# One kernel for banded attention, a Fourier mix and a feed-forward layer: the first batch's stores on three queues, and a new list schedule

## The chip, the cores and the metric

The kernel runs on one core of a Trainium2 chip. The metric is device time in microseconds, the median of several executions. Engines are named as in the profile: PE (TensorE, matmuls), PEld (its weight loads), DVE (VectorE), ACT (ScalarE), POOL (GpSimd), and SP (SyncE), which only issues transfers.

## What is computed

```python
# q, k, v: (8, 8, 576, 64) float32; w_ch1: (512, 2048); w_ch2: (2048, 512)
scores = q @ k.T / 8                      # per batch and head
mask_plain = (rel >= 0) & (rel < 32)                       # heads 0 to 3, rel = query - key
mask_dil = (rel >= 0) & (rel < 128) & (rel % 4 == 0)       # heads 4 to 7
x = softmax(where(mask, scores, -1e9)) @ v                 # -> (8, 576, 512), heads side by side
u = x + real(fft(fft(x, axis=1), axis=2))                  # along the sequence, then the channels
un = (u - mean(u)) / sqrt(var(u) + 1e-6)                   # along the channels
out = u + relu(un @ w_ch1) @ w_ch2
```

The weights come as 64-bit floats and are narrowed to 32 bits on the chip.

## The kernel before

**Stages.** For each of 8 batches: attention in four head pairs of two units each (`attend`; units are numbered 0 to 63, eight to a batch), where a unit multiplies queries and keys (line 681), masks and reduces on DVE (716), takes exponentials on ACT (722), transposes (736) and multiplies by the values (757, 770). Batch 0 begins with its dilated heads. Their scaled rows (`xt`, lines 797 and 801) are stored to DRAM in an order that folds the sequence (`xsp`, `xsm`, function `store`) and loaded back as half sequences (`fold`, line 570 for both). The plain heads of batch 0 stay in SBUF. `mix` then folds (lines 921 to 945, partly on POOL), multiplies by cosine and sine tables along the sequence (972, 994) and the channels (1018, 1024), adds (885, 887 on POOL), normalises (850 to 862) and writes the rows `us`. The tables' low halves are made on line 635.

Products are of 32-bit floats split in a high and a low part, so each takes three matmuls.

**Feed-forward.** The first 6 of 16 hidden blocks are a filler that runs beside attention and mix of later batches: `fill` takes pairs of row tiles through `up` (line 1152) and `down` (1168), with 12 weight tiles that `prep` loads and narrows (ACT 1090 and 1109, DVE 1092 to 1099, POOL 1111). The other ten blocks come last, as products of 2 x 2 blocks with fewer multiplications (lines 1434, 1532, 1499), ending with the rows left over in the last chunk (`late_down8`, `finish8`, DVE line 1518, `write_out`).

**What sets the order.** Every operation is handed to a `Plan` with an engine, an estimated cost, a priority (lower first) and what it reads and writes. `Plan.run` is a list schedule: it walks an assumed clock, and at each moment an engine takes the first of its ready operations by priority for which buffers are free. The order so found is written out per engine, and each engine runs its stream in order; the assumed times have no part in the program, only the order has. Priorities are built from the constants at the head of the file: a batch's attention lies at 12 b and above; `P_QK0`, `P_V0`, `P_ST0`, `P_FD0`, `P_MIX0` and `P_SPAN0` shift loads, stores, folded loads and mix of batch 0, `P_W` and `P_WF` the filler's 12 weight tiles, `P_FILL` and `P_FILLT` the filler itself. `Q_ST0` names the queues of batch 0's stores in turn (S for SP, A for ACT, P for POOL).

**Spins.** Where PE has nothing else by the planner's clock, it runs pairs of matmuls on a zero tile (line 605, priority 900, up to 250 pairs). Once the first bank of tag "ff" has been taken, the rest of them are dropped:

```python
            if o.prio == SPIN and turn["ff"]:
                o.cost, o.fn = 0.0, lambda: None
```

**Gangs.** PE changes its tiling between attention's score and value matmuls and all others. From unit `NG2` on the two units of a head pair issue their scores directly behind each other (`mate`), and their values too. From unit `NGANG` on a unit's scores also wait for the transposed copy of the unit two before.

## Time and profile before

| | |
|---|---|
| median of 3 runs (1012.09 to 1015.26) | 1012.46 us |
| the profiled execution: its time | 1010.0 us |
| its span, first to last instruction | 1008.2 us |
| PE busy | 997.2 us (99%) |
| DVE busy | 740.8 us (73%) |
| ACT busy | 480.3 us (48%) |
| POOL busy | 297.3 us (29%) |
| granted PE clock | 1.000 |

Busy times are unions of the instructions' spans; for PE the spins count as busy. Matmuls are pipelined, so one matmul's own duration is longer than the distance to the next.

### The profile page before, as it was taken

Reading aid. Unit: us, or ns where it says so; the run is one execution under the profiler, and the core shown is the slowest. Engines: PE = TensorE matmul, PEld = TensorE weight load, DVE = VectorE, ACT = ScalarE, POOL = GpSimd, SP = SyncE. Lnnn points to the kernel's source line nnn. Section 1 sums busy time; section 2 is a strip of 40 time slices with the busy share of each in tenths; the row PEclk is TensorE's granted clock in tenths of the full one; section 3 lists DMA queues with packets and bytes.
Section 4 is the critical chain, followed back from the end, with each engine's and each line's share of the span. In section 5 each row is a group of like instructions: output and inputs, shape, how many; then the busy total and the mean of one; then the engine's idle time right before and its main releaser. Section 6 shows DMA issues by size and latency. Waiting matters only on the chain.

```text
span 1008.2 us, 22155 instructions
## 1 busy us (share of the span) xinstructions
PE 997.2 (99%) x8381; PEld 893.3 (89%) x8381; DVE 740.8 (73%) x2131; ACT 480.3 (48%) x1190; POOL 297.3 (29%) x347
## 2 busy tenths in 40 slices
PE   9999999999999999999999999999999999999998
PEld 8888788989888999899898989899999999999987
DVE  5789987678777656978779776858585858585846
ACT  5776765465746332534435534344343535252522
POOL 1746563526253535474133301010010101010200
PEclk9999999999999999999999999999999999999999
DMA  9968678568864334525546032323232323232211
GB/s 323 305 176 245 206 222 223 161 169 227 225 189 125 113 106 111 168 74 168 158 135 189 32 74 95 74 95 74 87 81 84 85 84 84 84 85 84 84 63 42
DMA packets 92010, 136.31 MB, mean 135 GB/s; under 512 B 9598, under 2 KB 53871, under 8 KB 91904
## 3 DMA queue, kind: packets, MB, share of 16 engines
q1 hardware_dynamic: 88688, 126.77, 43.1%
q0 software_dynamic: 2688, 7.03, 2.3%
q8 instruction: 65, 1.06, 0.5%
q10 hardware_dynamic: 528, 1.11, 0.3%
q14 instruction: 41, 0.34, 0.1%
HBM read 97.66 MB, written 37.21 MB: 134 GB/s over the span
## 4 chain that ended last, share of the span: by engine, by line
PE 91%; DVE 5%; ACT 1%; issue 1%; POOL 1%; DMA 1%; DVEq 0%; SPq 0%; POOLq 0%; ACTq 0%
PE bank L1434 24%; PE bank L1532 20%; PE bank L1152 14%; PE bank L1168 13%; PE bank L1018 4%; PE bank L770 3%; PE bank L972 3%; PE bank L736 3%; PE bank L681 3%; PE bank L605 2%; PE bank L1499 1%; DVE pm L716 1%; PE bank L994 1%; DMA ut<-us 1%; ACT pm L722 1%
## 5 line engine op out<-in xcount | busy, mean ns | idle before, releaser
L1434 PE MATMUL bank<-low,wb 128*128 128x512 f32 x1080 | 255.6, 389 | 0.0
L1434 PEld LDWEIGHTS bank<-low,wb 128*128 128x128 f32 x1080 | 198.1, 188 | 36.9
L1152 PE MATMUL bank<-ut,low 128*128 128x256 f32 x1296 | 169.9, 283 | 0.3 <-DVE low L1160 0.2
L1152 PEld LDWEIGHTS bank<-ut,low 128*128 128x128 f32 x1296 | 159.2, 189 | 3.1 <-DVE low L1160 0.7
L1168 PE MATMUL bank<-low 128*128 128x512 f32 x648 | 161.0, 395 | 0.2 <-DVE low L1160 0.2
L1196 POOL DMA_INDIRECT ut<-us,flip_sb x20 | 41.1, 2053 | 375.1 <-DVE ut L1253 208.5
L1168 PEld LDWEIGHTS bank<-low 128*128 128x128 f32 x648 | 117.2, 188 | 22.9 <-DVE low L1160 0.7
L1440 ACT ACTIVATE xa<-bank 128x256 f32<-128x256 f32 x90 | 34.4, 382 | 177.7 <-PE bank L1434 177.7
L722 ACT ACTIVATE pm<-pm,mx 128x96 f32<-128x96 f32 x256 | 80.9, 368 | 40.3 <-DVE mx L716 39.3
L1471 DVE TENSOR_TENSOR y<-xa 128x384 f32<-128x384 f32 x45 | 25.1, 557 | 97.3 <-ACT xa L1440 97.0
L1275 DVE STREAM_TRANSPOSE ut<-ut 128x512 f32<-128x512 f32 (+1 forms) x76 | 70.6, 978 | 8.7 <-DMA ut<-us 8.5
L1242 DVE TENSOR_TENSOR ut<-ut,bank 128x512 f32<-128x512 f32 (+1 forms) x136 | 74.0, 553 | 2.1
L1160 DVE SCALAR_TENSOR_TENSOR low<-bank,low 128x256 fp32r<-128x256 f32 x108 | 45.1, 420 | 41.2 <-ACT low L1158 40.8
L1532 PEld LDWEIGHTS bank<-w2s,low 128*128 128x128 f32 x588 | 71.7, 188 | 2.1
L1158 ACT ACTIVATE low<-bank 128x256 fp32r<-128x256 f32 x108 | 41.2, 382 | 66.9 <-PE bank L1152 66.2
L1532 PE MATMUL bank<-w2s,low 128*128 128x256 f32 x588 | 72.1, 278 | 0.0
L716 DVE CUSTOM_DVE_ANT_0 pm<-bank,mask_sb 128x96 f32<-128x96 f32 x256 | 53.2, 249 | 14.9 <-PE bank L681 14.7
L1532 PEld LDWEIGHTS bank<-w2s,hm 128*128 128x128 f32 x483 | 58.9, 188 | 1.7
L1532 PE MATMUL bank<-w2s,hm 128*128 128x256 f32 x483 | 59.2, 278 | 0.0
L1109 ACT CAST low<-y 128x640 fp32r<-128x640 f32 (+1 forms) x50 | 35.8, 716 | 38.0 <-DVE y L1473 23.2
L1532 PE MATMUL bank<-low 128*128 128x256 f32 x420 | 51.5, 278 | 0.0
L1532 PEld LDWEIGHTS bank<-low 128*128 128x128 f32 x420 | 50.5, 188 | 0.8
(181 smaller groups left out, 1787.3 us busy)
## 6 DMA issues: line engine op xcount, KB each, us to landing
qk<-in_qk_dram SPq DMA_DIRECT2D x30, 576.0 KB
vt<-in_v_dram SPq DMA_DIRECT2D x31, 438.8 KB
us<-uc SPq DMA_DIRECT2D x36, 257.0 KB
part<-row SPq DMA_DIRECT2D x36, 256.0 KB
wst<-in_w_dram SPq DMA_DIRECT2D x18, 512.0 KB
ut<-us SPq DMA_DIRECT2D x36, 256.0 KB
ut<-part SPq DMA_DIRECT2D x36, 256.0 KB
ut<-us SPq DMA_DIRECT2D x64, 128.0 KB
```

The source lines that it names most:

```text
L716: nc.vector.tensor_tensor_reduce(prob(i)[ps_], sc()[e][ps_, KB * (i // 2):KB * (i // 2) + KB], mask_sb().bitcast(F32)[ps_, kind], -0.125, ...
L722: add("ACT", 0.265, lambda i=i: nc.scalar.activation(out=prob(i), in_=prob(i), func=AF.Exp, bias=mx()[:, i:i + 1], scale=-1.0), ((mx, i),) ...
L1018: nc.tensor.matmul(ps()[:n, :NEP], lhsT=ys[i]()[:, dt, a, rows], rhs=chn_sb[i]()[:, dt, c], start=(dt == 0 and x == 0), stop=(i == 1 and d ...
L1152: nc.tensor.matmul(z()[:, :n_tok], lhsT=wf()[a][:, kk], rhs=ut()[:, p, kk], start=(kk == 0 and n == 0), stop=(kk == KT - 1 and n == 2),)
L1158: add("ACT", act(n_tok) - 0.05, lambda: nc.scalar.activation(out=h()[:, 0, :n_tok], in_=z()[:, :n_tok], func=AF.Relu), (z,), ((h, 0),), prio)
L1160: add("DVE", dve(n_tok), lambda: nc.vector.scalar_tensor_tensor(h()[:, 1, :n_tok], z()[:, :n_tok], 0.0, h()[:, 0, :n_tok].bitcast(F32), op ...
L1168: nc.tensor.matmul(acc(), lhsT=h()[:, a, P * s:P * s + P], rhs=wf()[:, p], start=(first and n == 0), stop=(last and n == 2),)
L1196: add("POOL", 1.04, lambda: nc.gpsimd.indirect_dma_start(dst(), None, us[idx // 4](), bass.IndirectOffsetOnAxis(ap=flip_sb()[:, 4 * kk + i ...
L1242: add("DVE", dve(C if at in (outer, inner) else TOK1), lambda: nc.vector.tensor_tensor(out=blocks(part())[:, at], in0=blocks(part())[:, at ...
L1275: nc.vector.transpose(out=o[back], in_=x[:, g])
L1434: nc.tensor.matmul(z(), lhsT=wb1[NF1 + 2 * p + f]()[:, a, kk], rhs=ut()[:, x, kk], start=(kk == 0 and n == 0), stop=(kk == KT - 1 and n == 2),
L1532: nc.tensor.matmul(acc()[block // 2][:, TOK1 * (block % 2):TOK1 * (block % 2) + TOK1], lhsT=part(hl, a, i, i + 1), rhs=w2s[p]()[:, j, x], ...
```

## The change

The constants of the list schedule change, and with them the order of nearly everything ahead of the last ten hidden blocks. Batch 0's stores go by turns to POOL, ACT and SP. The seq tables' low halves move to DVE and the channel tables' to POOL (`TAB0`, `TAB1`: nonzero is DVE). The planner's assumptions on transfers change: POOL's start later and land later, and two transfers at a time slow each other by half of their overlap. Some assumed DVE costs rise. In the last chunk the second bank's products come in another order for the last pair of blocks (the whole-width product first), and its last DVE step is cut in two halves of 256 columns, each waiting only for its half of the bank.

```diff
-NPT2, NAV2 = 7, 13
-NGANG = 14
+NPT2, NAV2 = 7, 14
+NGANG = 16
-NMX, NG2 = 2, 36
-TAB0, TAB1 = 0, 3
+NMX, NG2 = 2, 32
+TAB0, TAB1 = 10, 0
-P_QK0, P_V0 = -22.11, 15.13
-P_ST, P_FD, P_WD, P_ST0, P_FD0, P_SPAN0, P_SPAN1 = -6.07, -50.32, -13.32, -9.18, -4.2, 26.34, 14.86
-P_QK, P_V, P_TR, P_MIX, P_SPAN, P_W, P_WF, P_FILL, P_FILLT = 19.35, 41.09, -71.2, -1.02, 10.19, 11.28, 7.1, 43.27, 10.96
-P_MIX0, P_MIX1 = -8.0, 6.45
-P_SEQ, P_CHN = 18.96, 20.71
-T_SEQ, T_CHN = 6.63, 39.16
-Q_ST0, Q_X0 = 'P', 'P'
+P_QK0, P_V0 = -28.96, -13.31
+P_ST, P_FD, P_WD, P_ST0, P_FD0, P_SPAN0, P_SPAN1 = -6.34, -52.48, 5.55, -21.88, 0.36, 3.04, 17.39
+P_QK, P_V, P_TR, P_MIX, P_SPAN, P_W, P_WF, P_FILL, P_FILLT = 15.62, 76.61, -97.91, -7.42, 0.09, 10.33, 7.1, 59.56, 47.29
+P_MIX0, P_MIX1 = -1.17, -2.08
+P_SEQ, P_CHN = 19.63, 37.65
+T_SEQ, T_CHN = 20.53, 34.77
+Q_ST0, Q_X0 = 'PAS', 'P'
...
-                        begin = max(pipe.get(eng, 0.0), end + 1.2)
+                        begin = max(pipe.get(eng, 0.0), end + ((LATE1 if lanes[eng] else LATE0) if eng == "POOL" else 1.2))
                         took = got.nbytes / (PIPE0 if end < T_PIPE else PIPE1)
-                        others = [x for x in pipe if x != eng and pipe[x] > begin]
-                        pipe[eng] = begin + took * (1 + len(others))
-                        for x in others:
-                            pipe[x] += took
-                        done = pipe[eng] + LAND[eng]
+                        pipe[eng] = begin + took
+                        for x in pipe:
+                            both = 0.5 * min(took, pipe[x] - begin)
+                            if x != eng and both > 0:
+                                pipe[eng] += both
+                                pipe[x] += both
+                        done = pipe[eng] + (LAND1 if eng == "POOL" else LAND0)
...
-LAND = {"SP": 1.6, "ACT": 1.6, "POOL": 2.8}
-PIPE0, PIPE1, T_PIPE = 3.2e5, 2.7e5, 55.0
+PIPE0, PIPE1, T_PIPE = 3.05e5, 2.7e5, 55.0
+LAND0, LAND1, LATE0, LATE1 = 0.8, 2.4, 4.5, 2.0
...
-            add("PE", 0.22, turn_over, (blank,), (spin,), SPIN, at=0.4 * n)
+            add("PE", 0.23, turn_over, (blank,), (spin,), SPIN, at=0.4 * n)
...
-            for n, (i, j, at) in enumerate((((0, 1, 1), (1, 0, 0), (4, 5, None)), ((2, 1, 1), (3, 0, 0), (5, 5, None)))[e]):
+            todo = [((0, 1, 1), (1, 0, 0), (4, 5, None)), ((2, 1, 1), (3, 0, 0), (5, 5, None))][e]
+            for n, (i, j, at) in enumerate(todo[2:] + todo[:2] if e and p == NPAIR - 1 else todo):
...
-            add("DVE", dve(C), lambda e=e, u=u, row=row: nc.vector.scalar_tensor_tensor(
-                blocks(row()), blocks(acc()[e])[:, ::-1], u()[:, C + 1:C + 2], blocks(row()), op0=ALU.mult, op1=ALU.add),
-                (uk, (acc, e)), (pk,), SOON)
-            write_out(idx + e, row, pk, prio)
+            if not e:
...
+            for x in (1, 0):
+                cols = slice(TOK1 * (1 - x), TOK1 * (1 - x) + TOK1)
+                hk = (f1, ("half", x))
+                add("DVE", dve(TOK1), lambda e=e, u=u, row=row, x=x, cols=cols: nc.vector.scalar_tensor_tensor(
+                    row()[:, cols], acc()[e][:, TOK1 * x:TOK1 * x + TOK1], u()[:, C + 1:C + 2], row()[:, cols], op0=ALU.mult, op1=ALU.add),
+                    (uk, pk, (acc, (e, x))), (hk,), SOON)
+            write_out(idx + e, row, ((f1, ("half", 0)), (f1, ("half", 1))), prio)
```

Four assumed DVE costs also change (0.075 to 0.12, 0.4 to 0.56, and 0.34 to 0.42 twice).

## Rows read from the trace of the kernel before

**Rows 1.** The page: span, and busy time of each engine.
```profile
span 1008.2 us, 22155 instructions
PE 997.2 (99%) x8381; PEld 893.3 (89%) x8381; DVE 740.8 (73%) x2131; ACT 480.3 (48%) x1190; POOL 297.3 (29%) x347
```
**Rows 2.** Table by stretch: length, busy us (instructions) by engine, clock, DMA share, GB/s.
```profile
84.00:350.00 266.00, 263.44 (x3035) 230.29 (x3034) 206.87 (x876) 150.94 (x427) 123.77 (x163) 1.00 0.67 190
350.00:990.00 640.00, 639.89 (x4116) 580.83 (x4115) 460.97 (x890) 271.01 (x601) 130.87 (x122) 1.00 0.34 98
```
**Rows 3.** Groups by line on PE: busy us, mean ns, idle before, releasers.
```profile
L605 PE MATMUL bank<-blank 128*128 128x220 f32 x234 | 36.6, 299 | 2.3 <-DVE blank L600 1.0 <-DVE y L978 0.6 <-DVE ut L878 0.4
```
**Rows 4.** Timeline of PE: start us, us, line, tiles, count.
```profile
83.96 1.30 PE L1152 MATMUL bank<-ut,low 128*128 128x256 f32 x9
```
**Rows 5.** The chain that ended last: start us, us, what.
```profile
9.10 0.22 PE bank L605 x2
...
982.70 7.26 PE bank L1532 x63
```
**Rows 6.** Table by stretch, of line 605 alone: PE and PEld busy (count).
```profile
0.00:40.00 40.00, 20.41 (x127) 17.85 (x128) 1.00 0.96 323
40.00:84.00 44.00, 16.24 (x108) 13.49 (x108) 1.00 0.66 202
```
**Rows 7.** Table by stretch, all instructions: PE, PEld, DVE, ACT, POOL.
```profile
0.00:40.00 40.00, 37.52 (x590) 32.97 (x591) 24.77 (x185) 25.27 (x73) 14.72 (x32) 1.00 0.96 323
40.00:84.00 44.00, 42.46 (x558) 37.00 (x558) 38.73 (x164) 31.24 (x87) 27.96 (x32) 1.00 0.66 202
84.00:115.00 31.00, 29.58 (x384) 24.61 (x383) 30.23 (x118) 22.08 (x61) 18.51 (x21) 1.00 0.84 242
```
**Rows 8.** Timeline of POOL: issues of batch 0's stores and loads, first fold.
```profile
21.91 0.61 POOL L570 DMA_DIRECT2D xsp<-xt  x1 [19.83 <-DVE mx L716]
...
31.39 0.54 POOL L570 DMA_DIRECT2D xsm<-xt  x1 [1.29 <-DMA xsm<-xt]
...
37.75 1.11 POOL L570 DMA_DIRECT2D x<-xsm  x2 [0.60 <-DMA xsm<-xt]
...
42.84 0.72 POOL L921 TENSOR_TENSOR t<-x,x 128x257 f32<-128x257 f32 x1
```
**Rows 9.** The chain that ended last, from 55 to 84 us.
```profile
55.92 1.17 DVE ut L1099
...
72.43 0.90 PE bank L605 x8
```
**Rows 10.** DMA issues from 20 to 45 us: count, KB each, median us to landing.
```profile
xsm<-xt POOLq DMA_DIRECT2D x1, 24.0 KB, 7.3
xsm<-xt POOLq DMA_DIRECT2D x1, 16.0 KB, 5.4
```
**Rows 11.** Timeline of DVE: last scaling, channel tables, a 256-column step, the last step.
```profile
22.96 0.49 DVE L797 TENSOR_TENSOR xt<-bank,rinv 128x320 f32<-128x320 f32 x1
...
61.30 1.29 DVE L635 TENSOR_TENSOR chn<-y,chn 128x516 fp32r<-128x516 f32 x2
...
993.98 0.42 DVE L1242 TENSOR_TENSOR ut<-ut,bank 128x256 f32<-128x256 f32 x1
...
1003.90 0.75 DVE L1518 SCALAR_TENSOR_TENSOR ut<-bank,ut 128x512 f32<-128x512 f32 x1 [0.65 <-PE bank L1499]
```
**Rows 12.** Timeline of SP's and ACT's queues: issues of loads.
```profile
0.72 0.41 ACTq L661 DMA_DIRECT2D qk<-in_qk_dram  x1
...
52.49 7.38 SPq L1089 DMA_DIRECT2D ut<-in_w_dram  x2
```
**Rows 13.** Groups by line on PE from 84 to 130 us.
```profile
L1168 PE MATMUL bank<-low 128*128 128x512 f32 x30 | 8.5, 408 | 0.2 <-DVE low L1160 0.2
```
**Rows 14.** Waits of PE's weight loads: total us, times, longest.
```profile
PEld bank L770 <- issue: 2.8, 12, 0.4
PEld bank L681 <- issue: 2.2, 10, 0.4
```

More of the change, by code (lines that the diff above doesn't have):

```diff
@@ L782, in of @@
             return av()[:, 65 * lo:65 * hi].rearrange("p (i d) -> p i d", d=65)
-        add("DVE", 0.075, lambda: nc.vector.tensor_scalar(
+        add("DVE", 0.12, lambda: nc.vector.tensor_scalar(
             sums()[:, 0:n], of(0, n)[:, :, D], 1e-9, None, op0=ALU.add), (av,), (sums,), prio)
@@ L851, in normalise @@
         add("DVE", 0.08, lambda: nc.vector.bn_aggr(out=uc()[:, C:C + 2], in_=stats()), (stats,), ((uc, 1),), prio)
-        add("DVE", 0.4, lambda: nc.vector.tensor_scalar(
+        add("DVE", 0.56, lambda: nc.vector.tensor_scalar(
             uc()[:, 0:C], u()[:, 0:C], uc()[:, C:C + 1], None, op0=ALU.subtract), ((u, 0), (uc, 1)), ((uc, 0),), prio)
@@ L1091, in narrow @@
             out=mag(), in_=flat(t, 0, 2 * C)[:, 1::2], func=AF.Abs), src, (m,), prio)
-        add("DVE", 0.34, lambda: nc.vector.tensor_scalar(mag(), mag(), F64_LOW, None, op0=ALU.max), (), (m,), prio)
-        add("DVE", 0.34, lambda: nc.vector.tensor_scalar(
+        add("DVE", 0.42, lambda: nc.vector.tensor_scalar(mag(), mag(), F64_LOW, None, op0=ALU.max), (), (m,), prio)
+        add("DVE", 0.42, lambda: nc.vector.tensor_scalar(
             bits(U32), flat(t, 2 * C, C, U32), 5, 2, op0=ALU.logical_shift_left, op1=ALU.logical_shift_right),
@@ L1212, in put @@
                     queues[e][0].dma_start(out=out[2 * pair_ + e, lo:lo + 32], in_=row()[p0:p0 + 32])
-                add(queues[e][1], 0.5, put, (done,), (), prio, 32 * 2048)
+                add(queues[e][1], 0.5, put, done, (), prio, 32 * 2048)
             return
@@ L1216, in write_out @@
             dma(lambda b=b, lo=lo, p0=p0, n=n: nc.sync.dma_start(
-                out=out[b, lo:lo + n], in_=row()[p0:p0 + n]), (done,), (), prio, n * 2048)
+                out=out[b, lo:lo + n], in_=row()[p0:p0 + n]), done, (), prio, n * 2048)
     def blocks(x):
@@ L1254, in finish_two @@
                 row(), row(), u(e)[:, C + 1:C + 2], u(e)[:, 0:C], op0=ALU.mult, op1=ALU.add), (uks[e],), (ps[e],), soon)
-            write_out(idx + e, row, ps[e], prio)
+            write_out(idx + e, row, (ps[e],), prio)
     def words(t):
@@ L1501, in late_down8 @@
                 key = "sum" if whole else "raw"
-                add("PE", 3 * pe(C if whole else TOK1), go, ((hl, (key, 0)), (hl, (key, 1)), w2s[p]), ((acc, e),),
-                    prio + 0.01 * e + 0.001 * n)
+                add("PE", 3 * pe(C if whole else TOK1), go, ((hl, (key, 0)), (hl, (key, 1)), w2s[p]),
+                    tuple((acc, (e, x)) for x in ((0, 1) if whole else (at,))), prio + 0.01 * e + 0.001 * n)
     def finish8(idx, acc, prio):
@@ L1517, in finish8 @@
                 row(), row(), u()[:, C + 1:C + 2], u()[:, 0:C], op0=ALU.mult, op1=ALU.add), (uk,), (pk,), prio)
-            add("DVE", dve(C), lambda e=e, u=u, row=row: nc.vector.scalar_tensor_tensor(
-                blocks(row()), blocks(acc()[e])[:, ::-1], u()[:, C + 1:C + 2], blocks(row()), op0=ALU.mult, op1=ALU.add),
-                (uk, (acc, e)), (pk,), SOON)
-            write_out(idx + e, row, pk, prio)
+            if not e:
+                add("DVE", dve(C), lambda e=e, u=u, row=row: nc.vector.scalar_tensor_tensor(
+                    blocks(row()), blocks(acc()[e])[:, ::-1], u()[:, C + 1:C + 2], blocks(row()), op0=ALU.mult, op1=ALU.add),
+                    (uk, (acc, (e, 0)), (acc, (e, 1))), (pk,), SOON)
+                write_out(idx + e, row, (pk,), prio)
+                continue
+            for x in (1, 0):
[5 more added lines that the diff above has]
+            write_out(idx + e, row, ((f1, ("half", 0)), (f1, ("half", 1))), prio)
     PRODUCTS = ((0, 0, 0, 0, True), (1, 1, 0, 3, True), (2, 5, 0, 2, False), (4, 6, 0, 1, False),
```

## The prediction

> **What bounds the kernel now.** I read the page first: TensorE is busy for 997.2 of 1008.2 us [rows 1]. So only three things can give time back: matmuls that do nothing, TensorE's own idle time, and the end. Then the table by stretch [rows 2]: from 350 to 990 us TensorE idles 0.11 us of 640, and nothing that a new order does there can help. It idles 2.56 us from 84 to 350, 4.0 before 84 [rows 7], and it has ended some 4 before the span does [rows 11]. Third, the costliest TensorE group of line 605 [rows 3]: 234 "spins" on a zero tile, which the order places wherever its forecast leaves TensorE nothing to do before the first feed-forward bank is taken. They all lie ahead of 84 us, where the first real feed-forward matmul of line 1152 starts [rows 4]; I call that moment T0. In the chain of work two spins take 0.22 us, 0.11 each [rows 5], so 234 take about 26 us: that is the large pot.
>
> How fast does the pot shrink if T0 comes earlier? From 40 to 84 us there are 108 spins [rows 6], 11.9 us, and the same stretch shows 1.54 us of idle TensorE [rows 7]: 13.4 of 44 us, 30.5%. The rest is real work (batch 1's attention, batch 0's mix) that must be done anyway. So 1 us off T0 is worth 0.305 us, as long as TensorE stays full behind T0.
>
> What holds T0? GpSimd's timeline [rows 8]: batch 0's dilated rows leave in 13 stores, the first issued at 21.91, the last at 31.39 us; the last loads of the folded rows wait for them until 37.75; the first fold starts at 42.84. Then the chain from 56 to 84 us [rows 9]: beside batch 0's mix it holds work that T0 does not need: weight narrowing (lines 1092 to 1099, 1109), batch 1's masks, exponentials and values, and spins. I add up 13.6 of the chain's 28 us as such work; the rows show the longest weight step and the longest run of spins. VectorE is the queue in which they meet: busy 38.73 of 44 and 30.23 of 31 us in the stretches from 40 to 115 [rows 7].
>
> **The change, part by part.**
>
> Three queues for the stores. Thirteen become five on GpSimd, five on ACT, three on SP. On GpSimd an issue takes about 0.54 us [rows 8], and by size its stores landed 5.4 to 7.3 us after it [rows 10]. The second half of the rows is ready at 23.36, when its scaling ends [rows 11]. Three GpSimd issues behind that end at about 25.1, so the last GpSimd store is in by 30.5 to 32.4 instead of 37.7, where the last load stopped waiting. That is 6 us, if the SP and ACT stores land no later. The trace has no landing for a store on those two; the transfer engines are 96% busy up to 40 us [rows 7], so below lies 0 (each store behind the bulk loads) and above about 10 (all in by 28). I take 6, since the five that stay on GpSimd set it.
>
> ACT gets five issues. The one issue on its queue took 0.41 us [rows 12], so 2 us of its sequencer, in a stretch, up to 40 us, in which it is busy for 25.27 [rows 7]: nothing, covered by the 14.7 that are free; without that cover, the 2 us.
>
> Priorities. Batch 0's mix had numbers spread from 4 to 30 and now lies between 10.8 and 13.9, ahead of nearly all of batch 1's attention (12 to 23) and of all weight tiles but the first. The gain is between 0 and the 13.6 us of foreign work in the chain. I take 6, a bit under half: the six "up" tiles must still be narrowed by VectorE before the first six products end, and what is pushed back still shares the engine. Together T0 comes 12 us earlier, from 84 to 72, between 0 and 24; 12 x 0.305 = 3.7 us, between 0 and 7.3.
>
> What is late next. Behind T0 VectorE has 0.77 us free in 31 and TensorE already idles 1.42 [rows 7]. Down matmuls of line 1168 come only 30 times from 84 to 130 us [rows 13], although a pair of row tiles needs 36: they wait for the second six weight tiles, whose priorities hardly change. The deferred attention is real work for that hole, so I charge 0.5 us, between 0 and 3.7 (all given back).
>
> Table splits. The seq tables' low halves go from GpSimd to VectorE, the channel tables' the other way. VectorE loses 1.29 us [rows 11] and gains 1.29 x 580/516 = 1.45, so 0.16 us more; GpSimd's share becomes smaller in the same ratio and moves to the stretch from 40 to 84 us, where it is free for 16 of 44 [rows 7]. Zero, and 0.16 x 0.305 if VectorE is the bound. The later seq load, the bank and gate counts (13 to 14, 14 to 16) and the costs that only the planner reads: no row prices them apart from the order; zero, with the stretch 84 to 350's 2.56 us of idle as the most that they can win and about as much that they can lose.
>
> More ganged pairs (from unit 32 on instead of 36). Two pairs more issue their scores, and their values, back to back: four entries into a tiling saved. Weight loads of the scores and the values stood without a visible releaser for 2.2 us in 10 cases and 2.8 in 12 [rows 14], about 0.22 each: at most 0.9, at least 0; I take 0.4, about half.
>
> The last VectorE step. It runs after the last matmul, 0.75 us on 512 columns; as two halves only the second remains behind TensorE, and 256 columns take 0.42 [rows 11]: 0.33 less. The first half needs a bank half that TensorE has finished three matmuls earlier (0.35 us: 63 of 256 columns take 7.26 [rows 5]), so it fits but for 0.07: 0.3.
>
> Sum: -3.7 + 0.5 - 0.4 - 0.3 = -3.9. The span goes from 1008.2 to 1004.3, the profiled execution from its 1010.0 to 1006.1. That execution lies 2.46 below the median of the runs shown, 1012.46; the median is what I forecast: 1008.6.
>
> **The rivals.**
>
> (a) Larger: T0 comes by the full 6 + 13.6 = 19.6 us earlier, 6.0 us, and V loads that come sooner lift the stage before 40 us too. There are 127 spins [rows 6] and 2.48 us of idle in it [rows 7], 16.5 of 40 us, 41%; 5 us less of it are 2.1. With the 0.7 of gang and tail: 8.8, 1003.7. For it: VectorE is free for 15.2 of these 40 us. Against it: the transfer engines, at 96%.
>
> (b) VectorE stays the bound: T0 comes early, and the time returns as idle TensorE between 72 and 130 us, because the sum of VectorE's work until then is the same. Only gang and tail are left: 1011.8. For it: 30.23 of 31 us; against it: VectorE is free for 5.3 us of the 44 ahead of T0, and feed-forward work asks little of it.
>
> (c) The stores gain issue time alone: eight of 13 leave GpSimd's stream, 8 x 0.54 = 4.3 us, not 6, because all queues drain through transfer engines that are 96% full. T0 moves by 10.3: 3.1 us instead of 3.7, 1009.2. The Trainium skill has this as a rule (DMA: Bandwidth & Descriptors, "Issuing engines are not separate DMA queues"): starting transfers from several engines saves only the sequencer's time to start them, since all share the same engines. No row here compares the queues at equal load.
>
> (d) Slower: ACT, which works in order, stands at one of its five stores. SP shows the price: two issues of weight tiles lasted 7.38 us [rows 12], where ACT's one took 0.41. If ACT's exponentials are held that long, each further link waits (masks' buffers, transposes, values), spins don't cover it since they are already in the order, and 7.4 - 3.9 makes 1016.0. It decides from a stand of 4 us on. Against it: ACT's queue carried one load before, and its stores are small.
>
> **How the numbers follow.** Chances: the forecast (2 to 6 us gained) 0.45, (a) 0.15, (b) 0.20, (c) 0.05, (d) 0.15. The range goes from 1001.2, which is (a) seen from the profiled execution's level (1010.0 - 8.8), to 1014.0, which holds (b) with some loss and leaves (d) out. By 0.3%, 3 us, about what a measurement of this kernel can tell from no change: faster are three quarters of the forecast's case, (a) and most of (c), 0.53; the same are the rest of these and nearly all of (b), 0.30; slower (d) and a little of (b), 0.17.
>
> **What would show it.** Stores: the fold's first GpSimd step near 36 us instead of 42.84. Priorities: line 1152's first matmul near 72. The pot: fewer than 200 spins, some 20 us or less of them. Behind T0: idle TensorE between T0 and 130 us near 2 us; if it is above 4, (b) holds. Tail: 0.42 us of VectorE behind the last matmul. The forecast is wrong if T0 moves by less than 5 us, if spins fall but idle time takes their place, or if ACT shows one long issue between 21 and 30 us.

## The result, and the profile of the changed kernel

The changed kernel is slower: 1019.38 us median (1017.73 to 1022.55) against 1012.28 us (1011.12 to 1015.26) of the kernel before on the same chip, a ratio of 1.0066, 95% interval 1.0046 to 1.0086. The forecast was 1008.6 us and the range ended at 1014.0; both the side and the range are missed.

Executions of one and the same kernel differ too: beside experiment 1 the kernel before ran 32 times, in 1009.42 to 1020.71 us, and the nine executions with a mean granted clock under 0.999 have a median of 1017.73 us, the other 23 one of 1013.12.

The profiled execution took 1020.76 us, its span is 1018.9, 10.7 more than before [rows 1]. The medians lie 7.1 apart: the profile of before is one of the kernel's shortest executions, so what follows explains somewhat more than the change cost. The first lines of its page give the span and each engine's busy time.

```profile
span 1018.9 us, 22102 instructions
PE 997.3 (98%) x8361; PEld 894.4 (88%) x8361; DVE 731.2 (72%) x2132; ACT 480.1 (47%) x1190; POOL 292.3 (29%) x339
```

TensorE is busy for as long as before, 997.3 us against 997.2. So by the page, what was lost is idle time of TensorE; that the busy time is equal is chance, as the clock below shows. The table by stretch says where the idle time is (length, then busy us and instructions of PE, PEld, DVE, ACT, POOL, then the granted clock, the DMA share and GB/s):

```profile
0.00:115.00 115.00, 107.30 (x1520) 94.03 (x1522) 91.43 (x474) 75.88 (x216) 54.67 (x74) 0.99 0.82 251
115.00:350.00 235.00, 229.79 (x2592) 201.69 (x2589) 168.64 (x736) 129.18 (x365) 105.85 (x146) 1.00 0.62 183
350.00:560.00 210.00, 205.91 (x1345) 186.11 (x1344) 153.59 (x324) 86.63 (x188) 87.96 (x96) 0.99 0.46 137
560.00:990.00 430.00, 430.00 (x2747) 390.24 (x2746) 301.08 (x567) 180.55 (x405) 43.83 (x25) 1.00 0.28 80
990.00:1019.00 29.00, 24.34 (x168) 22.30 (x166) 16.41 (x34) 7.90 (x18) 0.00 (x0) 1.00 0.16 45
```

Subtract the first number of PE from the length of its stretch, and do the same with [rows 2, 7]. TensorE idles 7.70 us up to 115 us (before 5.45), 5.21 from 115 to 350 (before 1.13) and 4.09 from 350 to 560 (before 0.11): +2.3, +4.1 and +4.0. The end costs 0.2 more. Before rounding that is 10.6 of the 10.7 us. So three things have to be explained, and two of them lie where the forecast saw nothing happen.

**Ahead of 40 us.** The engine that starts transfers works in order, and ScalarE's timeline (ACT, and ACTq for its transfer issues) shows it standing at its stores:

```profile
21.37 0.57 ACTq L572 DMA_DIRECT2D xsm<-xt  x1
22.49 0.28 ACTq L572 DMA_DIRECT2D xsm<-xt  x1
...
24.08 2.71 ACTq L572 DMA_DIRECT2D xsp<-xt  x2
27.58 0.52 ACTq L572 DMA_DIRECT2D xsm<-xt  x1
28.19 0.26 ACT L748 COPY ees<-bank 96x128 f32<-96x128 f32 x1 [4.46 <-DMA xsp<-xt]
```

ScalarE has been idle for 4.46 us before the copy out of TensorE's bank at 28.19 (line 748). An issue that is listed with x2 or x3 holds the waits between its transfers. On SP's queue the same happens at the three stores:

```profile
21.31 6.76 SPq L572 DMA_DIRECT2D xsm<-xt  x3
```

TensorE's timeline shows the price, and the chain of work shows what ended last: one transfer that clears a row, issued on SP at 18.42 and landed 9.14 us later.

```profile
28.51 1.61 PE L759 MATMUL bank<-vt,ees 96*64 96x65 f32 x40 [2.82 <-ACT ees L748]
```

```profile
18.42 9.14 DMA xsm<-blank
...
27.58 0.52 ACTq L572
```

ScalarE's store at 27.58 is of another piece than the cleared row; it starts 0.02 us after that row has landed (18.42 + 9.14 = 27.56). In the program's list of instructions, SP's and ScalarE's transfers take eight completion semaphores by turns, one list for both engines, and each transfer waits for the one eight places ahead of it. These are ScalarE's first transfers in that list:

```
L663 DMA qk_157<-in_qk_dram 128x1152
L572 DMA xsm_67<-xt 56x256 [waits DMAHW3_49,DVE_49]
L572 DMA xsm_67<-xt 40x256 [waits DMAHW4_49]
L572 DMA xsp_59<-xt_476 72x256 [waits DMAHW5_49,DVE_49]
L572 DMA xsp_59<-xt_476 72x256 [waits DMAHW7_49]
L572 DMA xsm_67<-xt_476 64x128 [waits DMAHW1_49]
```

The semaphores 3, 4, 5 and 7 belong to loads that SP has issued, 1 to the cleared row. The planner knows the limit of eight, but counts eight for each engine.

**The fold and T0.** The fold's first step starts at 42.68 us, 0.16 earlier than in [rows 8]; T0 lies at 90.72, 6.76 later than in [rows 4]. GpSimd's and TensorE's timelines:

```profile
30.32 1.10 POOL L572 DMA_DIRECT2D x<-xsp  x2 [4.47 <-DMA xsp<-xt]
...
42.68 0.72 POOL L923 TENSOR_TENSOR t<-x,x 128x257 f32<-128x257 f32 x1
```

```profile
90.72 1.31 PE L1154 MATMUL bank<-ut,low 128*128 128x256 f32 x9
```

**From 115 to 560 us.** TensorE's waits, by the line that waited and who released it (total us, times, longest), are many and short from 115 to 350; from 350 to 560 they are nearly all one:

```profile
PE bank L1154 <- DVE ve L856: 1.5, 1, 1.5
PE bank L1154 <- DVE ut L1297: 0.9, 1, 0.9
```

```profile
PE bank L1154 <- DVE low L1162: 3.8, 3, 2.4
```

The timeline around the longest of them, 525 to 538 us, has a slow step of GpSimd:

```profile
527.38 0.42 DVE L1095 TENSOR_SCALAR wst<-wst 128x512 uint32<-128x512 uint32 x1
527.53 4.17 POOL L1113 TENSOR_TENSOR wb<-wst,wb 128x512 fp32r<-128x512 f32 x1 [12.09 <-ACT wb L1111]
527.72 0.42 DVE L1095 TENSOR_SCALAR ut<-ut 128x512 uint32<-128x512 uint32 x1
...
531.73 0.33 SPq L1091 DMA_DIRECT2D wst<-in_w_dram  x1
532.01 1.29 POOL L1113 TENSOR_TENSOR wb<-wst,wb 128x512 fp32r<-128x512 f32 x1 [0.31 <-ACT wb L1111]
...
536.57 0.43 DVE L1094 TENSOR_SCALAR wst<-wst 128x512 f32<-128x512 f32 x1 [3.32 <-ACT wst L1092]
...
537.37 0.42 DVE L1162 SCALAR_TENSOR_TENSOR low<-bank,low 128x256 fp32r<-128x256 f32 x1
```

Read it forwards. GpSimd forms the low half of a late "up" tile (line 1113). The step takes 1.29 us a moment later, but 4.17 here, while VectorE works through two tiles' narrowing without a gap. The staging buffer "wst" comes free at 531.70; SP starts the next weight load into it at 531.73; VectorE, in order, waits 3.32 us for that weight, and the narrowing of the hidden row (line 1162) that TensorE needs stands behind it. TensorE waits 2.41 us; experiments 1 and 2, with the same order, show this wait again, with 2.50 and 2.41 us.

**The clock.** Behind its two longest waits, 2.82 us at 28.51 and 2.41 us at 537.84, TensorE is granted half of its clock, 1.2 GHz instead of 2.4. The table by stretch shows it (the third number from the end), and the matmuls do: of line 1154's, 51 take 6.00 us ahead of the second wait, and 21 take 4.27 us behind it.

```profile
30.00:33.00 3.00, 3.00 (x45) 2.74 (x43) 2.12 (x10) 1.86 (x6) 1.10 (x2) 0.50 0.91 276
539.00:541.00 2.00, 2.00 (x11) 2.00 (x11) 0.45 (x2) 1.17 (x3) 0.95 (x1) 0.50 0.00 0
```

```profile
529.42 6.00 PE L1154 MATMUL bank<-ut,low 128*128 128x256 f32 x51
537.84 4.27 PE L1154 MATMUL bank<-ut,low 128*128 128x256 f32 x21 [2.41 <-DVE low L1162]
```

Such stretches count as busy. The mean granted clock of this profile is 0.997, against 1.000 before: an estimated 3 us of the span (0.003 of 1018.9) that no table of idle time shows. Twenty spins fewer, an estimated 2.2 us, hide most of it in the sum of busy time.

**The end.** VectorE's timeline, to be held against the last of [rows 11]:

```profile
1012.99 0.75 DVE L1522 SCALAR_TENSOR_TENSOR ut<-bank,ut 128x512 f32<-128x512 f32 x1 [4.52 <-PE bank L1502]
1014.38 0.88 DVE L1530 SCALAR_TENSOR_TENSOR ut<-bank,ut 128x256 f32<-128x256 f32 x2 [0.64 <-PE bank L1502]
```

Both halves (x2) start after the last matmul has ended: 0.88 us behind TensorE instead of 0.75.

### The profile page after: what moved, and what is told of

Its sections match the earlier page's. It is cut to its first block, busy times and chain, and to the rows that moved or that the text cites. A ratio compares the mean times of both kernels' runs of the same rounds, so it can differ in the third digit from the quotient of the medians.

```text
span 1018.9 us, 22102 instructions
## 1 busy us (share of the span) xinstructions
PE 997.3 (98%) x8361; PEld 894.4 (88%) x8361; DVE 731.2 (72%) x2132; ACT 480.1 (47%) x1190; POOL 292.3 (29%) x339
## 4 chain that ended last, share of the span: by engine, by line
PE 84%; DMA 5%; DVE 4%; POOL 2%; issue 2%; ACT 1%; SPq 0%; DVEq 0%; ACTq 0%; POOLq 0%
PE bank L1436 24%; PE bank L1544 20%; PE bank L1170 11%; PE bank L1154 10%; PE bank L1020 3%; PE bank L772 3%; PE bank L974 3%; PE bank L683 3%; PE bank L738 3%; DMA us<-uc 3%; PE bank L607 2%; PE bank L1502 1%; DMA xsm<-blank 1%; DMA qk<-in_qk_dram 1%; DMA x<-xsm 1%
## 5 line engine op out<-in xcount | busy, mean ns | idle before, releaser
L1154 PE MATMUL bank<-ut,low 128*128 128x256 f32 x1296 | 172.2, 285 | 6.5 <-DVE low L1162 3.8
```

The source lines that it names most:

```text
L1154: nc.tensor.matmul(z()[:, :n_tok], lhsT=wf()[a][:, kk], rhs=ut()[:, p, kk], start=(kk == 0 and n == 0), stop=(kk == KT - 1 and n == 2),)
```

## The experiments

Sixteen kernels, each compared with the kernel before on its own chip. "Idle" is length less PE busy, in us, from the same table by stretch, in that kernel's one profiled execution.

| | kernel | ratio to before (95%) | idle 0-115 | 115-350 | 350-560 |
|---|---|---|---|---|---|
| | before, as in front | 1 | 5.45 | 1.13 | 0.11 |
| | changed | 1.0066 (1.0046-1.0086) | 7.70 | 5.21 | 4.09 |
| 1 | changed, cleared row by GpSimd | 1.0079 (1.0051-1.0106) | 8.24 | 5.09 | 3.67 |
| 2 | changed, stores by GpSimd | 1.0040 (1.0015-1.0065) | 5.62 | 4.22 | 3.19 |
| 3 | before, stores by turns | 1.0015 (0.9987-1.0043) | 7.28 | 0.91 | 0.11 |
| 4 | before, split last step | 1.0003 (0.9977-1.0029) | 7.72 | 1.60 | 0.11 |
| 5 | changed, old constants | 1.0081 (1.0051-1.0111) | 8.77 | 5.02 | 1.37 |
| 6 | changed, old planner costs | 1.0107 (1.0066-1.0148) | 7.49 | 5.43 | 2.22 |
| 7 | before, new constants | 1.0066 (1.0044-1.0089) | 6.12 | 3.15 | 1.89 |
| 8 | changed, late low halves on VectorE | 1.0014 (0.9991-1.0036) | 7.81 | 3.58 | 1.26 |
| 9 | changed, 2 and 8 and old last step | 1.0014 (0.9995-1.0033) | 6.71 | 4.85 | 2.15 |
| 10 | before, late low halves on VectorE | 1.0007 (0.9984-1.0030) | 7.10 | 2.30 | 0.00 |
| 11 | before, new planner costs | 1.0135 (1.0103-1.0167) | 8.77 | 8.49 | 3.47 |
| 12 | changed, planner counts shared slots | 1.0057 (1.0036-1.0077) | 5.72 | 2.60 | 3.26 |
| 13 | before, numbers nudged, first signs | 0.9979 (0.9957-1.0001) | 5.40 | 0.53 | 0.60 |
| 14 | before, numbers nudged, second signs | 1.0114 (1.0071-1.0156) | 7.85 | 5.59 | 2.39 |
| 15 | changed, nudged, first signs | 1.0053 (1.0031-1.0075) | 8.99 | 5.61 | 1.73 |
| 16 | changed, nudged, second signs | 1.0077 (1.0050-1.0104) | 10.72 | 5.74 | 1.78 |

Spins count as busy: 234 before, 214 in the changed kernel, but 262, 276 and 278 in experiments 6, 7 and 12, so there some of the loss hides among them. And idle time up to 115 us varies by itself: experiment 4 has the order of before in this stretch, and 2.3 us more of it. Stretches at half clock are not in the idle time either: the mean granted clock of the profiled execution is 0.993 in experiment 5, 0.996 to 0.997 in 1, 2, 6, 14, 16 and the changed kernel, 0.998 or more in the others, and 1.000 in 7, 9 and 13; in some of them a part of that stretch lies behind the last matmul, where it costs nothing.

The theory after the first reading: ScalarE and SP stand because they share slots (A), and the rest of the loss comes of the order that the planner now writes (C). Rivals: the stand comes of the stores' own queue or data (B), or the early stand delays everything behind it.

### 1. The cleared row of batch 0 goes through GpSimd

```diff
-            dma(lambda b=b: nc.sync.dma_start(
+            dma(lambda b=b: (nc.sync if b else nc.gpsimd).dma_start(
```

> The changed kernel with its order kept; only batch 0's zero row goes out by GpSimd instead of SP. In the changed kernel ACT stands from 24.1 to 28.2 us at its stores, the last of which waits for the completion slot that the zero row holds until 27.56. Theory A (SP's and ACT's transfers share eight completion slots in turn, so each ACT store waits for whatever transfer stands eight before it, mostly bulk loads): now the slot before is that of the V load issued at 18.0 us, which lands at about the same time, so ACT stands until 26 to 28 us all the same and the time stays within 1.5 us of the changed kernel. Rival B (the zero row alone is slow): the stand ends by 25 us, TensorE's idle time before 40 us falls from 5.9 to some 3 us and the time by 2.5 to 3.5 us.

ScalarE still stands; in its timeline only the piece differs:

```profile
23.65 3.02 ACTq L572 DMA_DIRECT2D xsp<-xt  x2
27.99 0.51 ACTq L572 DMA_DIRECT2D xsm<-xt  x1
28.60 0.26 ACT L748 COPY ees<-bank 96x128 f32<-96x128 f32 x1 [5.16 <-DMA vt<-in_v_dram]
```

1021.63 us. The cleared row was only the one that happened to come last; without it one of SP's loads ends the wait, the V load that the last row names. TensorE idles 6.48 us before 40 us, where B asked for some 3. That speaks for shared slots and against that row as the cause.

### 2. The changed kernel's order, all 13 stores started by GpSimd

```diff
-            send("S" if b else Q_ST0[n % len(Q_ST0)], ..., early, P * 2048 // len(put))
+            send("S" if b else Q_ST0[n % len(Q_ST0)], ..., early, P * 2048 // len(put), None if b else nc.gpsimd)
```

> The changed kernel with its order kept; all 13 stores of batch 0's dilated rows are issued by GpSimd, as before the change. Both early theories: no ACT stand, no SP stand of 6.8 us, TensorE's idle time before 40 us falls from 5.9 to 2.5 to 3.5 us. Theory C (the idle time from 115 to 550 us, 9.3 against 1.3 us before, comes from the new order itself): it stays at 7 to 10 us, and the time falls by 2 to 4 us only, to 1015 to 1017. Rival D (it is the early stand, passed on by engines that run in order): it falls below 4 us as well and the time comes to 1009 to 1012.

1019.11 us, 1.0040. Neither ScalarE nor SP stands, and idle time up to 115 us is back at 5.62; before 40 us it is 4.46, more than the 2.5 to 3.5 expected. The fold starts at 41.89 us, no later than with three queues. But 7.4 us of idle TensorE from 115 to 560 are still there, as theory C says. The intervals of this kernel and the changed one overlap, so what the early stand costs in time is not resolved; the idle time shows that the stand is not where most of the loss lies.

### 3. The order of before, its stores started by turns

```diff
+            ..., None if b else (nc.gpsimd, nc.scalar, nc.sync)[n % 3])
```

> The kernel before with its order kept; its 13 stores are issued by turns by GpSimd, ACT and SP, where the order has GpSimd issue them. Theory A: the ACT and SP stores wait behind bulk loads in the shared completion slots, ACT and SP stand for 2 to 6 us between 21 and 35, TensorE idles 1 to 4 us more before 60 us, and the time is 0 to 4 us longer. Rival (the stores leave sooner and nothing stands): the first fold starts 4 to 6 us before 42.84, but as the order is the same the time stays within 1 us.

1016.66 us, 1.0015, not to be told from no change. ScalarE is idle for 2.04 us behind one of its stores, and TensorE idles 1.55 us more than before ahead of 60 us, both at the lower end of what theory A asked for. The fold's first step of GpSimd starts at 44.18 us, not the 4 to 6 us earlier of the rival. With the order and the queue of before it starts at 42.84 in [rows 8] and at 45.25 in experiment 4:

```profile
44.18 0.72 POOL L922 TENSOR_TENSOR t<-x,x 128x257 f32<-128x257 f32 x1
```

The one part of the change that was to give 6 us of T0 gives nothing alone. From 115 to 560 us this kernel idles 1.02 us: with the old order the loss there is gone.

### 4. The split last step alone

> The kernel before with the change's tail alone: the last pair's whole-width product first and the last VectorE step in two halves. The prediction's term: 0.3 us less behind the last matmul, VectorE's last step 0.42 instead of 0.75 us; the time within the noise (0 to 0.5 us less). Rival: the halves or the other order of products cost TensorE a wait, 0.3 us or more longer.

The edit is the change's hunks on the last chunk. 1013.08 us, 1.0003, which can't tell 0.3 us. VectorE's last entry can:

```profile
1009.99 0.87 DVE L1528 SCALAR_TENSOR_TENSOR ut<-bank,ut 128x256 f32<-128x256 f32 x2 [0.64 <-PE bank L1500]
```

The first half was declared to need only its half of the bank, but it starts directly ahead of the second, 0.64 us after VectorE's previous step and after the last matmul. So the split only adds: the two halves last 0.87 us where the whole step lasts 0.75. The Trainium skill has a sentence that bears on this (PSUM — Partial Sum Buffer, "The four PSUM rules"): for XLA's own matmuls the compiler's back end serialises two engines' accesses to one bank and quadrant. These rows look the same, but no run shows that this is the reason here; which part of the tools held the first half was not tried.

### 5 to 7. The parts of the new order

Experiment 5 is the changed kernel with the priorities, due times, counts and table splits of before; 6 has the planner's pipe, landing and step costs of before; 7 is the kernel before with the change's constants and nothing else.

> The changed kernel with all priorities, times, gang and bank counts of before; it keeps the three queues, the planner's new assumptions and the tail. Theory C (the new constants make the order whose idle time from 115 to 550 us is 9.3 us): it falls below 4 us, T0 stays near 86 to 90, and the time is that of before plus the queues' 1 to 3 us, 1014 to 1016. Rival (the planner's new assumptions on transfers make that order): it stays above 6 us and the time at 1017 or more.

> The changed kernel with the planner's old assumptions on transfers and costs; it keeps the new constants, the three queues and the tail. Theory C: idle TensorE from 115 to 550 us stays above 5 us, the time at 1017 to 1022. Rival (the planner's new assumptions make the order): it falls below 4 us and the time below 1016.

> The kernel before with the new constants alone (one queue, the old planner, the old tail). Theory C: idle TensorE from 115 to 550 us comes to 5 us or more, T0 does not come below 80, and the time is 3 to 8 us above that of before. Rival, the prediction's own step (the priorities are worth 6 us of T0 and only queues or planner spoil it): T0 at 80 or less and the time 1 to 3 us below that of before.

1021.56, 1025.74 and 1020.69 us: 1.0081, 1.0107, 1.0066. Experiment 7 came out as theory C has it, and 6 in its idle time (7.65 us from 115 to 560), though it is slower than expected; 5 came out by its rival, with 6.39 us idle from 115 to 560 and a time above 1017. So it is not the constants alone that make an order which loses: the planner's new costs make one too. The parts do not add up. New constants alone cost as much as the whole change; taking them out leaves the loss as it is, though in experiment 5's profile an estimated 7 us of the span (0.007 of 1020.6) are half clock. Experiment 7 has 276 spins, and its first feed-forward matmul at 91.13 us, where the forecast had it 6 us earlier than before:

```profile
91.13 0.62 PE L1152 MATMUL bank<-ut,low 128*128 128x256 f32 x3
```

### 8. The low halves of the last ten up tiles on VectorE, the changed order kept

```diff
-                prep_up(f, wb1[f], stage(0), (gate1,) if f < split else (gate1, gate2), FILL + f)
+                prep_up(f, wb1[f], stage(0), (gate1,) if f < split else (gate1, gate2), FILL + f, via=nc.vector)
```

> The changed kernel with its order kept; the low halves of the last ten up tiles are made by VectorE at the places where the order has GpSimd make them. In the changed kernel one such GpSimd step beside a run of VectorE steps lasts 4.17 us instead of 1.29, the next weight load leaves at 531.7, ACT and VectorE stand for it with two evacuations behind, and TensorE idles 2.41 us at 537.8. Theory E (that step's length is what makes the load late): the 2.41 us vanish or fall below 0.5, idle TensorE from 350 to 560 us falls from 4.1 to 1 to 2 us, the time by about 2 us. Rival (the load is late for another reason, or VectorE's own extra 0.7 us a tile comes in the way): the idle time stays at 3 us or more.

1014.91 us, 1.0014: the interval ends below where that of the changed kernel begins. The table by stretch of this kernel, and the same stretch of the changed one:

```profile
490.00:560.00 70.00, 70.00 (x418) 62.16 (x417) 53.44 (x98) 33.03 (x70) 13.09 (x12) 1.00 0.55 159
```

```profile
490.00:560.00 70.00, 67.59 (x399) 60.30 (x398) 48.47 (x85) 31.12 (x64) 22.92 (x18) 0.98 0.53 150
```

From 490 to 560 us TensorE has no gap left. VectorE's step takes 0.69 us each time (10 steps, 6.9 us in all), where GpSimd's took 1.29 to 4.17. That accounts for 2.8 us of idle time from 350 to 560. The granted clock of the stretch rises from 0.98 to 1.00 with it: the half clock behind the wait is gone too, an estimated 1.4 us (0.02 of 70). Together they come to 4.2 us, of some 5 us of time where 2 were expected. Another 1.6 us of idle time between 115 and 350 went as well, where nothing was edited, so the time has more in it than this step: one wait there (line 1154 on "ve") is 1.51 us in the changed kernel's profile and 0.48 in this one.

### 9. The changed order with its three faults taken back

> The changed kernel's order with three places taken back: the 13 stores are started by GpSimd, the low halves of the last ten up tiles are formed on VectorE, and the last step is whole again. Theory (the loss sits in stands of the new order, each with its own price): the changed kernel's 7 us over before, less about 4.5 (late low halves) and 2 (stores), gives 1.000 times before, 0.997 to 1.002; ScalarE shows no transfer issue over 0.8 us between 20 and 30 us, idle TensorE 40 to 560 us falls under 5 us, and the step of VectorE behind the last matmul is 0.75 us. Rival (the two gains overlap, or one of them was chance): 1.003 or more. If the new order had any gain of its own behind its stands, the ratio would be under 0.997.

1015.94 us, 1.0014. The time is as expected and VectorE's last step is 0.75 us again, but the sum behind it is not: idle time from 40 to 560 us is 10.1 us, not under 5, and taking the stores back brings nothing that can be seen on top of experiment 8. The intervals of both reach some 2 us to either side, so a price of 2 us for the early stand is neither shown nor ruled out.

### 10. The same edit as 8 on the old order

> The old order with the low halves of the last ten up tiles on VectorE, nothing else. Theory (in the new order GpSimd's slow step lies on the path of the weights, in the old one it is covered): TensorE was idle 0.11 us between 350 and 560 us, so there is nothing to gain, 0.998 to 1.002 times before. Rival (VectorE's shorter step is a gain of 4 us in any order): 0.996 or less. A second rival (VectorE is the tighter engine there, 160 of 210 us busy): 1.003 or more.

1015.88 us, 1.0007: nothing to gain, as there was no gap. But the theory's reason, a slow step that is covered, is not what the profile of before shows: its ten GpSimd steps of this kind take 1.29 to 1.74 us, and none is slow. The longest:

```profile
455.32 1.74 POOL L1111 TENSOR_TENSOR wb<-wst,wb 128x512 fp32r<-128x512 f32 x1
```

So both belong to the new order: that a step takes 4.17 us, and that a weight load waits for it.

### 11. The planner's new costs alone

> The kernel before with the planner's new assumptions alone (late landings of GpSimd's transfers, shared pipe, four costs); constants, stores and last step as before. If the parts simply add up (stores alone +3 us, constants alone +7, all together +7), the planner alone would have to bring 3 us: 0.997. If the old order is one that any fresh plan loses (planner with the stores by turns cost 8 us, stores in the old order 1.5 to 3), it costs about 5 us: 1.005, with 2 to 4 us of idle TensorE between 115 and 560 us where before has 1.2. This tells whether the late landings were worth planning for.

1026.93 us, 1.0135, the slowest of all. The costs are nearer to the measured durations (0.42 for the narrowing step that takes 0.42) and the plan made with them is worse than expected by both branches. Its waits from 115 to 560 us are spread over six lines of the kernel; the three longest sums are:

```profile
PE bank L1154 <- DVE low L1162: 2.8, 4, 1.3
PE bank L738 <- ACT pm L724: 2.3, 3, 1.6
PE bank L683 <- DVE mx L718: 1.7, 1, 1.7
```

### 12. The planner counts SP's and ScalarE's transfers in one list

```diff
-            if o.nbytes and len(lanes[o.eng]) >= 8 and lanes[o.eng][-8] > now:
+            slot = lanes["SP" if o.eng == "ACT" else o.eng]
+            if o.nbytes and len(slot) >= 8 and slot[-8] > now:
...
-                        lanes[eng].append(done)
+                        lanes["SP" if eng == "ACT" else eng].append(done)
```

> The changed kernel, but the planner counts SP's and ScalarE's outstanding transfers in one list of eight, as the program's waits do, in place of eight for each. Theory (ScalarE stood because the plan did not know that it shares slots with SP's bulk loads): the plan then places ScalarE's stores where a slot is free, no issue of ScalarE takes over 1 us between 20 and 35 us, TensorE's 2.8 us wait for the copy out of its bank is gone, idle 20 to 40 us falls from 2.8 to 2 us or less. Rival (the stand comes of the store's data or of the queue itself): an issue of 2 us or more remains. The rest of the order is planned anew with it, so the time itself is only bounded: 1.001 to 1.009 times before.

ScalarE's issues in this kernel:

```profile
29.73 0.57 ACTq L573 DMA_DIRECT2D xsm<-xt  x1
31.83 0.28 ACTq L573 DMA_DIRECT2D xsm<-xt  x1
32.16 0.34 ACTq L573 DMA_DIRECT2D xsp<-xt  x1
36.79 0.35 ACTq L573 DMA_DIRECT2D xsp<-xt  x1
37.76 0.51 ACTq L573 DMA_DIRECT2D xsm<-xt  x1
```

No stand is left; the plan now puts the stores 8 to 12 us later, where slots are free. The list of waits above and experiment 1 show A, and this agrees: the stand is the wait for a shared slot, and a plan that knows of it avoids it. TensorE idles 1.00 us from 20 to 40 us, below the 2 expected. The time is 1020.12 us, 1.0057, no better than the changed kernel's: the fold now starts at 49.39 us, and there are 278 spins.

### 13 to 16. Neighbours of both kernels

The 24 priorities and due times each moved by 0.4 us up or down and nothing else, twice for each kernel, for example:

```diff
-P_MIX0, P_MIX1 = -8.0, 6.45
+P_MIX0, P_MIX1 = -7.6, 6.85
```

> The kernel before with each of its priorities and due times moved by 0.4 us up or down (first choice of signs), nothing else. Theory S (the order before is the best of many that lie near it, and any fresh order brings stands of its own): slower, 1.003 to 1.010, with 2 to 6 us of idle TensorE between 115 and 560 us in place of 1.2. Rival (the constants of the change are bad in themselves and a small nudge is harmless): 0.998 to 1.002, idle there under 2 us.

> As the first nudge of the kernel before, with another choice of signs. Theory S: 1.003 to 1.010 and 2 to 6 us idle between 115 and 560 us. Rival: 0.998 to 1.002 and under 2 us.

> The changed kernel with each of its priorities and due times moved by 0.4 us (first choice of signs), nothing else. If its order is an ordinary one among its neighbours, the neighbour lies about it, 1.004 to 1.012 times before. If the changed constants were the best of their neighbourhood, it is slower than the changed kernel's 1.0066 by 0.003 or more. If the changed order is an unlucky one, the neighbour is at 1.003 or less, and what is lost is chance.

> As the first nudge of the changed kernel, with another choice of signs: 1.004 to 1.012 times before if its order is an ordinary one among its neighbours, 1.010 or more if it was the best of them, 1.003 or less if it was an unlucky one.

1011.83, 1025.12, 1019.45 and 1022.11 us. The two neighbours of before lie 13.3 us apart: 0.9979 and 1.0114. This is neither of the two answers that I had written down: one nudge is harmless, as the rival says, and the other costs as much as the whole change or more (the intervals overlap), as theory S says. The tables by stretch of these two, 115 to 350 and 350 to 560 us:

```profile
115.00:350.00 235.00, 234.47 (x2679) 206.12 (x2678) 171.59 (x761) 131.50 (x371) 102.02 (x140) 1.00 0.65 187
350.00:560.00 210.00, 209.40 (x1332) 187.89 (x1331) 157.70 (x312) 84.00 (x184) 90.28 (x98) 1.00 0.43 130
```

```profile
115.00:350.00 235.00, 229.41 (x2649) 199.90 (x2648) 168.69 (x756) 131.48 (x373) 99.69 (x135) 0.99 0.63 182
350.00:560.00 210.00, 207.61 (x1355) 187.58 (x1354) 157.17 (x322) 84.42 (x183) 96.74 (x108) 1.00 0.48 138
```

The slow one idles 7.98 us there, the other 1.13. Its longest wait is a new one, on GpSimd, and behind it the granted clock is half again (0.50 from 120 to 123 us):

```profile
117.68 0.80 PE L972 MATMUL bank<-tail_sb,eot 128*128 128x290 f32 x4 [2.68 <-POOL eot L943]
```

Both neighbours of the changed kernel lie about it, 1.0053 and 1.0077: its order is an ordinary one among those near it.

## Why the prediction was wrong, step by step

Two steps failed. T0 did not come the 12 us earlier that were to bring 3.7 us, and the work behind T0, charged with 0.5 us, lost 6.6 us of TensorE's time in waits, and more in the clock behind them.

**What bounds the kernel.** Spins, idle time and the end are what can be won, and the idle time and the end hold 10.6 of the 10.7 us. What can be lost is more: the granted clock was 1.000, and a stretch without idle time can only lose. I wrote that from 350 to 990 us "nothing that a new order does there can help". True, and I read from it that the stretch was out of play; it lost 4.0 us of idle time and an estimated 1.4 of clock. That it idled 0.11 us of 640 was a property of one order.

**"Three queues for the stores": 6 us of T0.** Measured: the fold 0.16 us earlier in the changed kernel, 1.3 later in experiment 3, both within what one order shows from one execution to another (42.84 and 45.25). I gave the bound (nothing, if each store goes behind the bulk loads) and chose 6 of 10, because the five stores left on GpSimd seemed to set it. The wait came from a place I had not looked at: slots shared with SP's bulk loads. Rival (c), with the Trainium skill's rule ("DMA: Bandwidth & Descriptors", "Issuing engines are not separate DMA queues"), was the better judge of these stores: starting them from other engines did not bring the fold sooner. Not even the 4.3 us of issue time that (c) allows were saved. A slip in the same step had no effect: the scaling in [rows 11] ends at 23.45 us, not 23.36.

**Rival (d): ScalarE stands at a store.** It happened, and as described: 4.5 us, above the 4 us from which it was to decide, with SP's 6.8 beside it. But its price was wrong. I took 7.4 us of a stand as 7.4 of time; experiment 2 takes the stand away and gets 2.1 us of idle time back ahead of 115 us, and in experiment 9 no gain can be seen. So (d) named a mechanism that is there, and not the cause of most of the loss; that its 1016.0 lies nearer to the measured time than any other figure is luck, since neither the 7.4 nor the 3.9 in it was there.

**"Priorities": 6 us of T0.** No gain in any profile. With the constants alone T0 is 91.13 us, without the stand (experiment 2) 89.57, and never under 87.97 with new constants (experiment 9); four profiles of the old order have it between 83.96 and 89.86. Moving the mix ahead in the list of priorities did not move it on the engines. The priorities decide only between steps that are ready at the same moment. Why the mix is not ready sooner was not traced; each of these orders has its own chain up to T0.

**1 us of T0 is worth 0.305 us.** Not refuted, and not shown. T0 came 6.76 us later, which makes 2.1 us by the rule. Up to T0, spins at 0.11 us and idle TensorE hold 31.2 us instead of 29.8, which is 1.5 more: 3.7 more idle, 2.2 less of spins. But experiment 4's T0 differs by 5.9 us with the same order, so one profile of each can't confirm a rate.

**"What is late next": 0.5 us, 0 to 3.7.** The mis-sized term, and the one that decides. From 84 to 560 us TensorE idles 6.6 us more than before (9.30 against 2.67), all of it behind 130 us: from T0 to 130 it idles 1.45, so neither the hole that I charged for nor rival (b) showed. The upper bound was exceeded too, since it was only what T0 could give back. The bound should have come from the number of hand-overs that a fresh order arranges anew, not from the gain. Part of it is found: the late low halves on GpSimd (experiment 8: 2.8 us of idle time and an estimated 1.4 of clock shown, some 5 us of time in all). The rest, from 115 to 350 us, is one wait of 1.5 us and many under 1, and its cause stays open. Experiments 13 and 14 suggest why no one part has it: moving numbers by 0.4 us brings as much or as little.

**The planner's costs: "zero".** I called them costs that only the planner reads, with 2.56 us of idle time as the most to win "and about as much" to lose. They are the largest single part, 1.35% alone (experiment 11), and that part disappears among the others when all are changed together.

**Gang: 0.4.** No gain shows. Weight loads of the scores and the values stood 3.2 and 3.2 us in 22 cases in the changed kernel's profile, 2.2 and 2.8 in 22 before [rows 14].

**The last step: 0.3.** Wrong in sign: +0.13 in the changed kernel, +0.12 in experiment 4. The half was free by the tile's bookkeeping but not in the trace. And a half takes 0.48 us there, not the 0.42 of the other 256-column step that I took for it, so 0.27 would have been the most.

**What stays open.** Whether the constants or the planner's new costs are worse in themselves than those of before. One of two nudges of the kernel before costs 1.1%, between what the constants (0.7%) and the planner's costs (1.35%) cost alone, and two nudges are too few to say how such orders are spread. No version here beats the kernel before: the nearest, experiment 13, has an interval that still holds 1.

## What to carry to other kernels

When a change touches the inputs of a planner that writes the whole order, its price is first that of a new order: here kernels with the same work, and numbers moved by 0.4 us, lay 1.3% apart, so a sum of local gains of 0.4% can't decide, and the stretch with no idle time is the one that has most to lose. Judge a local idea with the order held (as experiments 2, 3, 8 and 10 do) before planning anew. And before moving a transfer to an idle queue, ask what it shares with the busy one: its slots, not only its engines. Count a long wait of TensorE with the clock behind it: here the table of idle time left out an estimated 3 us.

## What the runs showed of the hardware and the tools

A step of GpSimd on 128 x 512 numbers took 1.29 us, and 4.17 us where it started beside a run of VectorE steps that narrow two tiles back to back: the run ended at 530.55 us, the step at 531.70. In other overlaps GpSimd's step took 1.29 us and VectorE's was the long one, 1.55 us instead of 0.42:

```profile
428.67 1.29 POOL L1113 TENSOR_TENSOR wb<-wst,wb 128x512 fp32r<-128x512 f32 x1 [0.30 <-ACT wb L1111]
428.69 1.55 DVE L1095 TENSOR_SCALAR wst<-wst 128x512 uint32<-128x512 uint32 x1
```

The Trainium skill has a rule for it (SBUF — State Buffer, "Who interferes with whom"): some steps of VectorE, those with two inputs in SBUF among them, contend with GpSimd for a port pair that both use and only one can hold. These rows agree, in that one of the two engines stands; no run here separates the kinds of VectorE step.

A transfer on a queue that was idle waited for another queue's transfer, since both take their completion semaphores from one list of eight: ScalarE's two stores 2.71 us, SP's three 6.76, against 0.28 to 0.57 for one that doesn't wait.

The stage before T0 is not the same from one execution to the next: with the order of before, experiment 4's first feed-forward matmul started at 89.86 us, 5.9 later than in [rows 4], and TensorE idled 2.3 us more up to 115 us. From 46 to 48 us its granted clock was 0.50, where the profile of before has 1.00 from 40 to 84 [rows 7]. So T0 in one profile is no measure of an edit to within some us.

```profile
89.86 1.32 PE L1152 MATMUL bank<-ut,low 128*128 128x256 f32 x9
```
